# Attention's last steps in the middle of layer 1's slots, masks in three pieces, 25 products of zeros in place of 55

## The chip, the cores and the metric

The kernel runs on one core of a Trainium2 chip. The metric is device time in microseconds (us). The engines named here are PE (TensorE, matrix products; PEld is its weight load), DVE (VectorE), ACT (ScalarE), POOL (GpSimd) and SP (SyncE, which issues most of the DMAs). A line such as L615 is a line of the kernel before.

## The reference

Attention with sink keys and a sliding window, then two dense layers, all in float32 (B=2, H=8, S=768, D=64; window 128, 4 sink keys; d_model 512, d_ff 2048):

```python
scores = q @ k.T / sqrt(D)
keep   = (pos_k < n_sink) | ((rel >= 0) & (rel < window))
a      = softmax(where(keep, scores, -1e9))        # sum + 1e-9
x      = (a @ v).transpose(0, 2, 1, 3).reshape(1536, 512)
h = x @ w_in                                       # layer 1: 512 -> 2048 -> 512
P = a0 + a1*h + a2*h**2 + a3*h**3
Q = 1 + abs(b0)*abs(h) + abs(b1)*h**2
x = (P / (Q + 1e-6)) @ w_out
h = maximum(x @ w_in2, 0)                          # layer 2
out = (h * h) @ w_out2
```

n_sink and window are read at run time, so the masks are built on the chip.

## The kernel before, in words

**Arithmetic.** Every float32 operand of a large product is split into a rounded high half and a low half (names ending in h and l), and a product is three products of halves: high by high, high by low, low by high. The high half is made by ACT, the low half is the difference, made by DVE or POOL. The weights come as 64-bit numbers, packed; DVE turns a tile of them into float32 in three integer steps (L234, L240, L246: the weight conversion), and `w_fin` splits it (L267 on ACT, L268 on POOL).

**Attention.** 12 units of 128 tokens (6 for each batch entry) by 4 pairs of heads make 48 steps, n = 0 to 47, in a software pipeline. Step n issues: the exponentials of step n-1 (`expo`, ACT L434); the scores of step n (L404), ahead of which come some products of zeros (`fill`, L532) into the same PSUM tile; the masked maximum of those scores (DVE: from unit 1 on a predicated copy L410, then L417, which adds a mask m_0, m_1 or m_2); the transposes of step n-2's exponentials (`trans`, L454) and their copies with the window's triangles (POOL L463, L467); the product with v of step n-4 (`pv`, L494), and, every fourth step, the sink keys' share (L501, L503), the division (L506), the sink columns' transpose (`sinks_t`, L477) and, some steps later, the transposes of the finished unit (`xt`, L358) with its split into xh and xl (ACT L276, DVE L277). The scores lie in a PSUM tag S of two buffers, so the first product of step n+2, a zero where there is one, can start only when L417 of step n has read its tile. The table DENSE holds the number of zeros ahead of the scores of steps 0 to 11, DENSE_B that of steps 24 to 27, where the second batch entry begins. Another 14 stand ahead of everything (NW0).

**Masks.** `setup_first` makes m_0 (for unit 0), `setup_rest` the other masks: tri for L410, m_1 for unit 1 on and m_2. Its operations stand on DVE in step 0, behind the scores of that step. The helper `addm` is line 100. The split of q and k (`split`, L364 and L365) leaves the low half of unit 1 to DVE, that of later units to POOL. In step 1 POOL builds the block-diagonal mask bd of the sink values (`diagonal`, L329 and L333).

**Layers.** Layer 1 is computed in slots, one for each step k over tiles of d_ff and chunks of 512 tokens. Slot k issues in this order: the split of the function's value of k-2 (`act_c`: gh on ACT L672, gl on POOL L673), up to two `w_fin`, the rational function of k-1 (`act_b`), the first product of k+1 (`g1`, L615: 12 products of 512 columns into a PSUM tile T), ACT's and POOL's share of the function of k (`act_a`), the weight conversion until a due count (`w_until(due(k))`), and the second product of k-2 (`g2`, L690, 12 products into the S tiles). T has two buffers: g1(k+1) can start only when L653, the first DVE operation of `act_b` of k-1, has read g1(k-1)'s tile. `act_b` also has gaps in which up to one conversion step each is put on DVE. The list of what each engine executes is the order in which these functions issue.

**The seam.** The first chunks of x are finished before the last unit is. So g1(0) is issued in step 46, and in the steps NP+k (NP = 48) for k = 0 to 5 the whole slot k follows the product with v (`ahead`, L583). Steps 48 to 53 hold no scores of their own; they hold the last exponentials, transposes, products with v and `xt`: unit 10's in step 49, unit 11's in step 53, behind slot 5. Those `xt` and the sink transposes take the PSUM tag U, which the function's quotient (L657, L658) uses too. Weight conversion goes on in U until step 51's end, then in tag O. From slot 6 on, slots follow one another.

Of the kernel before, what the change touches and what calls it, by code (L numbers as in the profile page):

```python
# [15 lines left out]
P = 128  # L16
SK = 8
# [1 line left out]
TWO32 = 4294967296.0  # L19
WS = 3  # L20
NW0 = 14
DENSE = (4, 5, 6, 6, 4, 4, 3, 3, 2, 2, 2, 2)
DENSE_B = 3
QP = 1.0 + 1e-6

LEAST = 2.0 ** -15 * 1.125
# [12 lines left out]
def kernel(  # L39
# [59 lines left out]
    def addm(dst, src):  # L99
        nc.vector.tensor_scalar(out=dst, in0=src, scalar1=-1.0, scalar2=BIG, op0=ALU.add, op1=ALU.mult)  # L100
# [35 lines left out]
    def setup_rest(rel, win, snk, tmp, m_1, m_2, tri):  # L136
        nc.vector.tensor_scalar(out=tri, in0=rel[:, P:], scalar1=0.0, scalar2=None, op0=ALU.is_lt)
        nc.vector.tensor_tensor(out=tmp, in0=win[:, 0:P], in1=win[:, P:], op=ALU.max)
        for m in (m_1, m_2):
            addm(m[:, 0:P], tmp)  # L140
        addm(m_2[:, P:], snk[:, 0:SK])
        nc.vector.tensor_tensor(out=tmp[:, 0:SK], in0=snk[:, 0:SK], in1=win[:, 0:SK], op=ALU.is_gt)
        addm(m_1[:, P:], tmp[:, 0:SK])

    def setup_moe():
        nc.scalar.mul(out=na, in_=ab[:, 0:4], mul=-1.0)
# [21 lines left out]

    wst = {"load": 0, "int": 0, "fin": 0}
    wraw, wx, wt = {}, {}, {}  # L170
    conv = {"tag": "U"}
    NW = 2 * NF
    spare = [f"b{j}" for j in range(NW - 2 * NCH)]
    parts = {}
# [75 lines left out]
            w_load()  # L250

    def w_until(steps):
        while wst["int"] < min(steps, len(todo)):
            j, i = todo[wst["int"]]
            if jobs[j][0] == "c" and i == WS - 1 and len(wx) == 2:
                return
            w_step()
# [31 lines left out]
    def ps_t(tag=None, tail=False):  # L289
        if tail:  # L290
            return ps_s()[:, 0]
        if tag is None:
            tag = "U" if hq else "T"
        return ps.tile([P, 512], F32, tag=tag, name=tag, bufs=2 if tag == "T" else 1)


    def attention(ap, extra, ahead):
        kh = ap.tile([P, NPR, NS, BS], F32R, name="kh")
        kl = ap.tile([P, NPR, NS, BS], F32R, name="kl")
        m_0 = ap.tile([P, P], F32, name="m_0")  # L300
# [51 lines left out]
            nc.gpsimd.tensor_tensor(out=l, in0=m, in1=h.bitcast(F32), op=ALU.subtract)  # L352
            vs[b] = (h, l)

        def transposed(t):
            d = ps_t()
            for pr in range(NPR):
                nc.tensor.transpose(  # L358
                    d[:, pr * P:(pr + 1) * P], t[:, 2 * pr:2 * pr + 2, :].rearrange("p h d -> p (h d)"), ident
                )  # L360
            return d.rearrange("p (r t) -> p r t", r=NPR)

        def split(u, h, l, d, r=slice(0, NPR)):
            nc.scalar.copy(out=h[:, r], in_=d[:, r])  # L364
            (nc.vector if u == 1 or r.stop <= 2 else nc.gpsimd).tensor_tensor(  # L365
                out=l[:, r], in0=d[:, r], in1=h[:, r].bitcast(F32), op=ALU.subtract
            )

# [104 lines left out]
        def sinks_t(u):  # L473
            if u not in sk:
                return
            sd = ps_t()
            nc.tensor.transpose(sd[:, 0:P], sk.pop(u).rearrange("p j h s -> p (j h s)"), ident)  # L477
            st = ap.tile([P, P], F32R, name="st", bufs=2)
            hf = H * SK
            nc.scalar.copy(out=st, in_=sd[:, 0:P])  # L480
            nc.vector.tensor_tensor(out=st[hf:], in0=sd[hf:, 0:P], in1=st[hf:].bitcast(F32), op=ALU.subtract)
            sT[u] = st
# [33 lines left out]

        def xt(u):
            c, t0 = u // UPC, (u % UPC) * P
            d = transposed(ops.pop(("x", u)))
            split_ps(xh[c][:, :, t0:t0 + P], xl[c][:, :, t0:t0 + P], d)  # L520

        NP = NU * NPR
# [22 lines left out]
        prep_q(0, first)  # L545
        next(masks)
        prep_k(0, first)
        for n in range(NP + 6):
            u, pr = divmod(n, NPR)
            if 0 <= n - 1 < NP:  # L550
                expo(n - 1)
            if n < NP:
                scores(n)
            if n == 0:
                prep_q(0, second)
                prep_k(0, second)
                prep_q(0, others)
                prep_k(0, others)
                setup_rest(*next(masks), m_1, m_2, tri)
                sink_keys(0)  # L560
            if n == 1:
                bd = diagonal()
                moe = setup_moe()
            if pr == 0 and u + 2 < NU:
                load(u + 2)
            if pr == 1 and n < NP and u % NB == 0:
                load_sinks(u // NB)
            if 9 <= n < 20:
                next(moe, None)
            if 0 <= n - 2 < NP:  # L570
                trans(n - 2)
            if 0 <= n - 1 < NP and pr == 0:
                sinks(n - 1)
            if n >= 6 and pr == 2 and n // 4 - 1 < NU:
                sinks_t(n // 4 - 1)
                sums(n // 4 - 1)
            if 12 <= n <= NP and pr == 0:
                xt(n // 4 - 3)
            if n == NP + 1:
                xt(NU - 2)  # L580
            if 0 <= n - 4 < NP:
                pv(n - 4)
            if n in ahead:  # L583
                ahead[n]()
            if pr == 0 and u + 1 < NU:
                prep_q(u + 1)
            if pr == 1 and u + 1 < NU:
                prep_k(u + 1)
            if pr == 2 and u % NB == 0 and 0 < u < NU:
                sink_keys(u)  # L590
            if n in (5, NB * NPR + 3):
                sink_values(u // NB, bd)
            if n in (7, NB * NPR + 4):
                sink_split(u // NB)
            if n == NP + 5:
                xt(NU - 1)
            extra(n)

    def half(L, g):
# [21 lines left out]
    def layers(mp, due):  # L623
# [118 lines left out]

        K = len(steps)

        def slot(k):
            if 0 <= k - 2:
                act_c(k - 2)
            w_fin()
            w_fin()
            if 0 <= k - 1 < K:  # L750
                act_b(k - 1, lambda: w_until(min(due(k), wst["int"] + 1)))
            if k + 1 < K:
                g1(k + 1)
            if k < K:
                act_a(k)
            split_late()
            w_until(due(k))
            if 0 <= k - 2:
                g2(k - 2)
            if k == K + 1:  # L760
                finish(0)
                finish(1)
# [272 lines left out]
    with tc.tile_pool(name="ap", bufs=1) as ap:  # L1035
        def extra(n):
            if n == 3:
                for _ in range(NWR):
                    w_load()
            w_fin()  # L1040
            if n % 4 != 2:
                w_until(min(WS * NA, (WS * NA * (n - 4)) // (NU * NPR - 9)))
            if n == NU * NPR + EARLY - 1:
                conv["tag"] = "O"

        attention(
            ap, extra, {NU * NPR - 2: lambda: g1(0)} | {NU * NPR + k: lambda k=k: slot(k) for k in range(EARLY + 2)}
        )
    wp2 = main.enter_context(tc.tile_pool(name="wp2", bufs=1))
    wpool += [wp2] * (NW - NA)  # L1050
    for n in range(EARLY + 2, slots):
        slot(n)
        if n == KL + 3 * NF - 3:
            fl = verdict(mp)
# [43 lines left out]
```

## Time and profile before

| | |
|---|---|
| median of 3 runs | 664.74 us (663.9 to 664.88) |
| profiled execution, its own time | 662.6 us |
| span of that execution, first to last instruction | 660.9 us |
| mean granted TensorE clock | 0.996 of full speed |
| PE busy | 643.5 us, 97% of the span |
| DVE, ACT, POOL busy | 435.8, 365.5, 351.4 us |
| idle time of L615 behind L653 (whole span) | 6.4 us |

The time of the profiled execution is 1.7 us above its span, and 2.1 us below the median of the runs. Busy times are of instructions; PE's ends are modelled, and neighbouring matrix products overlap in the records, so that starts are to be compared rather than ends.

### The profile page before, as it was taken

Reading aid. Unit: us, or ns where it says so; the run is one execution under the profiler, and the core shown is the slowest. Engines: PE = TensorE matmul, PEld = TensorE weight load, DVE = VectorE, ACT = ScalarE, POOL = GpSimd, SP = SyncE. Lnnn points to the kernel's source line nnn. Section 1 sums busy time; section 2 is a strip of 40 time slices with the busy share of each in tenths; the row PEclk is TensorE's granted clock in tenths of the full one; section 3 lists DMA queues with packets and bytes.
Section 4 is the critical chain, followed back from the end, with each engine's and each line's share of the span. In section 5 each row is a group of like instructions: output and inputs, shape, how many; then the busy total and the mean of one; then the engine's idle time right before and its main releaser. Section 6 shows DMA issues by size and latency. Waiting matters only on the chain.

```text
span 660.9 us, 9330 instructions
## 1 busy us (share of the span) xinstructions
PE 643.5 (97%) x3189; PEld 525.5 (80%) x3189; DVE 435.8 (66%) x885; ACT 365.5 (55%) x783; POOL 351.4 (53%) x353
## 2 busy tenths in 40 slices
PE   8999999898999999999999999999999999999995
PEld 6788788776888888888888888888888888888884
DVE  5687786485989798867667679959766242441231
ACT  4788886755888778868759744333332132222220
POOL 4777785345776757667649547444443222222221
PEclk9999999999999999999999999999999999999998
DMA  7846642022322233212111135737637354430101
GB/s 196 228 117 174 168 114 65 0 64 64 97 94 66 96 96 96 64 33 64 32 33 32 64 127 171 247 110 248 222 122 250 97 190 128 144 111 1 63 1 69
DMA packets 64375, 72.06 MB, mean 109 GB/s; under 512 B 15424, under 2 KB 55360, under 8 KB 64320
## 3 DMA queue, kind: packets, MB, share of 16 engines
q1 hardware_dynamic: 64176, 71.38, 35.2%
q8 instruction: 27, 0.44, 0.3%
q14 instruction: 28, 0.23, 0.1%
q10 hardware_dynamic: 144, 0.00, 0.0%
HBM read 68.23 MB, written 3.15 MB: 108 GB/s over the span
## 4 chain that ended last, share of the span: by engine, by line
PE 92%; DVE 3%; issue 1%; POOL 1%; ACT 1%; DMA 1%; DVEq 0%; POOLq 0%; ACTq 0%
PE s L690 40%; PE T L615 33%; PE U L615 7%; PE O L494 5%; PE s L404 3%; PE T L454 2%; PE s L532 2%; DMA raw<-in_spans_dram 1%; PE O L503 1%; PE T L358 0%; DVE t L653 0%; PE O L501 0%; POOL w L268 0%; DVE ql L365 0%; ACT pe L434 0%
## 5 line engine op out<-in xcount | busy, mean ns | idle before, releaser
L615 PE MATMUL T<-xh,w 128*128 128x512 f32 x640 | 211.7, 392 | 6.4 <-DVE t L653 6.4
L673 POOL TENSOR_TENSOR gl<-g,gh 128x512 fp32r<-128x512 f32 x48 | 62.2, 1297 | 161.4 <-ACT gh L672 161.4
L615 PEld LDWEIGHTS T<-xh,w 128*128 128x128 f32 x640 | 120.2, 188 | 34.2 <-DVE t L653 7.6
L690 PE MATMUL s<-gh,w 128*128 128x512 f32 x384 | 126.2, 390 | 0.0
L615 PE MATMUL T<-xl,w 128*128 128x512 f32 x320 | 125.5, 392 | 0.0
L690 PE MATMUL s<-w,gh 128*128 128x512 f32 x384 | 119.6, 392 | 0.0
L673 POOL TENSOR_TENSOR gl<-t,gh 128x512 fp32r<-128x512 f32 x48 | 62.3, 1299 | 48.3 <-ACT gh L672 42.2
L636 POOL TENSOR_TENSOR t<-t,ah 128x512 f32<-128x512 f32 x48 | 62.3, 1297 | 48.2 <-ACT t L633 45.7
L690 PEld LDWEIGHTS s<-w,gh 128*128 128x128 f32 x384 | 72.0, 188 | 16.4
L268 POOL TENSOR_TENSOR w<-wx,w 128x512 fp32r<-128x512 f32 x64 | 83.1, 1300 | 2.9 <-ACT w L267 2.9
L690 PEld LDWEIGHTS s<-gh,w 128*128 128x128 f32 x384 | 72.1, 188 | 15.7
L672 ACT CAST gh<-g 128x512 fp32r<-128x512 f32 x48 | 29.9, 622 | 84.2 <-PE s L690 78.7
L690 PE MATMUL s<-w,gl 128*128 128x512 f32 x192 | 75.3, 392 | 0.0
L690 PE MATMUL s<-gl,w 128*128 128x512 f32 x192 | 75.2, 392 | 0.0
L615 PEld LDWEIGHTS T<-xl,w 128*128 128x128 f32 x320 | 60.1, 188 | 12.4
L661 DVE SCALAR_TENSOR_TENSOR t<-t,U 128x512 f32<-128x512 f32 x48 | 33.0, 687 | 30.1 <-ACT U L658 30.0
L672 ACT CAST gh<-t 128x512 fp32r<-128x512 f32 x48 | 29.8, 622 | 40.4 <-DVE t L665 32.4
L647 DVE TENSOR_TENSOR g<-r,T 128x512 f32<-128x512 f32 x32 | 21.8, 684 | 45.1 <-ACT r L640 45.1
L640 ACT ACTIVATE r<-T 128x512 f32<-128x512 f32 x32 | 19.2, 599 | 54.3 <-PE T L615 54.3
L494 PE MATMUL O<-vr,ph 128*128 128x64 f32 x352 | 44.7, 268 | 0.1
L494 PEld LDWEIGHTS O<-vr,ph 128*128 128x128 f32 x352 | 43.2, 192 | 0.4 <-issue 0.3
L434 ACT ACTIVATE pe<-ns,nmax 128x136 f32<-128x136 f32 (+1 forms) x96 | 38.3, 401 | 9.1 <-DVE nmax L417 8.6
(151 smaller groups left out, 1152.3 us busy)
## 6 DMA issues: line engine op xcount, KB each, us to landing
wr<-in_w_in_dram SPq DMA_DIRECT2D x54, 512.0 KB, 3.8
wr<-in_w_out_dram SPq DMA_DIRECT2D x52, 512.0 KB, 3.8
qr<-in_q_dram SPq DMA_DIRECT2D x12, 256.0 KB, 4.1
kr<-in_k_dram SPq DMA_DIRECT2D x12, 256.0 KB, 4.5
vr<-in_v_dram SPq DMA_DIRECT2D x12, 256.0 KB, 4.9
wr<-in_v_dram SPq DMA_DIRECT2D x6, 512.0 KB, 4.8
out_dram<-part SPq DMA_DIRECT2D x12, 256.0 KB, 2.1
vsc<-in_v_dram SPq DMA_DIRECT2D x4, 16.0 KB
```

The source lines that it names most:

```text
L268: nc.gpsimd.tensor_tensor(out=t[:, 1], in0=xf, in1=t[:, 0].bitcast(F32), op=ALU.subtract)
L404: nc.tensor.matmul(d[e][:, 0:w].rearrange("p (j n) -> p j n", n=bw), lhsT=ql[a][s, pr, :], rhs=kk[b][s, pr, slots, 0:bw], start=(a + b == ...
L434: nc.scalar.activation(out=t[:, e, 0:w], in_=ns[e][:, 0:w], func=ACTF.Exp, scale=-1.0, bias=nmax[:, ix:ix + 1], accum_out=rs[:, 2 * pr + e ...
L494: nc.tensor.matmul(o[:, h * D:(h + 1) * D], lhsT=pt[:, j, e], rhs=ld[u - 1 + j, "v"][:, h, :], start=(h == 0 and j == (i == 0)), stop=Fals ...
L615: nc.tensor.matmul(h, lhsT=wi[a][:, kk * P:(kk + 1) * P], rhs=(xh, xl)[b][c][:, kk, :], start=(kk == 0 and a + b == 0), stop=(kk == KD - 1 ...
L636: nc.gpsimd.tensor_tensor(out=t, in0=t, in1=ah, op=ALU.mult)
L640: nc.scalar.activation(out=r, in_=h, func=ACTF.Relu)
L647: nc.vector.tensor_tensor(out=g, in0=st.pop(k), in1=h, op=ALU.mult)
L661: nc.vector.scalar_tensor_tensor(out=t, in0=t, scalar=QP, in1=r0, op0=ALU.add, op1=ALU.mult)
L672: nc.scalar.copy(out=gh, in_=g)
L673: nc.gpsimd.tensor_tensor(out=gl, in0=g, in1=gh.bitcast(F32), op=ALU.subtract)
L690: nc.tensor.matmul(acc[L, g, c][m], lhsT=lh, rhs=rh, start=(f == f0 and a + b == 0), stop=(f == f1 and a == 1),)
```

## The change

**Slots and steps.** The loop over steps ends at 47. Slots 0 to 4 then each get a function `mid` that issues step NP+j after g1(j+1) and `act_a(j)`, and before the conversion and g2(j-2). g1(0) stays in step 46. xt of unit 11 is issued in step 52 in place of 53, into tag O; xt of unit 10 stays in step 49, and unit 11's sink transpose moves from step 50 to 49, and both go into tag S. Weight conversion is switched off from the end of step 48 to the end of step 52. The plain slots begin with 5.

**Masks.** `setup_rest` is a generator of three pieces, one each in steps 0, 1 and 2; m_2's first part is copied from m_1. `diagonal` and `setup_moe` move from step 1 to 2, the sink values from step 5 to 6 and their split from 7 to 8. The low halves of unit 1's q and k go to POOL.

**Zeros.** DENSE and DENSE_B are smaller: 2, 3, 3, 2 fewer in steps 1 to 4; 2, 1, 1, 2, 2, 2, 2 fewer in steps 5 to 11; 2 fewer in each of steps 24 to 27.

```diff
 NW0 = 14
-DENSE = (4, 5, 6, 6, 4, 4, 3, 3, 2, 2, 2, 2)
-DENSE_B = 3
+DENSE = (4, 3, 3, 3, 2, 2, 2, 2)
+DENSE_B = 1
 QP = 1.0 + 1e-6
...
         nc.vector.tensor_tensor(out=tmp, in0=win[:, 0:P], in1=win[:, P:], op=ALU.max)
-        for m in (m_1, m_2):
-            addm(m[:, 0:P], tmp)
-        addm(m_2[:, P:], snk[:, 0:SK])
+        yield
+        addm(m_1[:, 0:P], tmp)
         nc.vector.tensor_tensor(out=tmp[:, 0:SK], in0=snk[:, 0:SK], in1=win[:, 0:SK], op=ALU.is_gt)
         addm(m_1[:, P:], tmp[:, 0:SK])
+        yield
+        nc.vector.tensor_copy(m_2[:, 0:P], m_1[:, 0:P])
+        addm(m_2[:, P:], snk[:, 0:SK])
 
     def setup_moe():
...
-        while wst["int"] < min(steps, len(todo)):
+        while conv["on"] and wst["int"] < min(steps, len(todo)):
             j, i = todo[wst["int"]]
...
             nc.scalar.copy(out=h[:, r], in_=d[:, r])
-            (nc.vector if u == 1 or r.stop <= 2 else nc.gpsimd).tensor_tensor(
+            (nc.vector if r.stop <= 2 else nc.gpsimd).tensor_tensor(
                 out=l[:, r], in0=d[:, r], in1=h[:, r].bitcast(F32), op=ALU.subtract
...
                 return
-            sd = ps_t()
+            sd = ps_t(tail=u == NU - 1)
             nc.tensor.transpose(sd[:, 0:P], sk.pop(u).rearrange("p j h s -> p (j h s)"), ident)
...
             c, t0 = u // UPC, (u % UPC) * P
-            d = transposed(ops.pop(("x", u)))
+            d = transposed(ops.pop(("x", u)), ps_t("O") if u == NU - 1 else ps_t(tail=u == NU - 2))
             split_ps(xh[c][:, :, t0:t0 + P], xl[c][:, :, t0:t0 + P], d)
...
         prep_k(0, first)
-        for n in range(NP + 6):
+        bd, moe, rest = None, None, None
+
+        def step(n):
+            nonlocal bd, moe, rest
             u, pr = divmod(n, NPR)
             if 0 <= n - 1 < NP:
                 expo(n - 1)
@@ -556,9 +560,11 @@
                 prep_k(0, second)
                 prep_q(0, others)
                 prep_k(0, others)
-                setup_rest(*next(masks), m_1, m_2, tri)
                 sink_keys(0)
-            if n == 1:
+                rest = setup_rest(*next(masks), m_1, m_2, tri)
+            if n < 4:
+                next(rest, None)
+            if n == 2:
                 bd = diagonal()
                 moe = setup_moe()
             if pr == 0 and u + 2 < NU:
@@ -571,7 +577,7 @@
                 trans(n - 2)
             if 0 <= n - 1 < NP and pr == 0:
                 sinks(n - 1)
-            if n >= 6 and pr == 2 and n // 4 - 1 < NU:
+            if (n >= 6 and pr == 2 and n < NP) or n == NP + 1:
                 sinks_t(n // 4 - 1)
                 sums(n // 4 - 1)
             if 12 <= n <= NP and pr == 0:
@@ -580,22 +586,26 @@
                 xt(NU - 2)
             if 0 <= n - 4 < NP:
                 pv(n - 4)
-            if n in ahead:
-                ahead[n]()
+            if n == NP - 2:
+                g1(0)
             if pr == 0 and u + 1 < NU:
                 prep_q(u + 1)
             if pr == 1 and u + 1 < NU:
                 prep_k(u + 1)
             if pr == 2 and u % NB == 0 and 0 < u < NU:
                 sink_keys(u)
-            if n in (5, NB * NPR + 3):
+            if n in (6, NB * NPR + 3):
                 sink_values(u // NB, bd)
-            if n in (7, NB * NPR + 4):
-                sink_split(u // NB)
-            if n == NP + 5:
+            if n in (8, NB * NPR + 4):
+                sink_split(u // NB if n > 8 else 0)
+            if n == NP + 4:
                 xt(NU - 1)
             extra(n)
 
+        for n in range(NP):
+            step(n)
+        for j in range(5):
+            slot(j, lambda: step(NP + j))
 
 
     def half(L, g):
@@ -742,7 +752,7 @@
 
         K = len(steps)
 
...
                 act_a(k)
+            mid()
             split_late()
...
                 w_until(min(WS * NA, (WS * NA * (n - 4)) // (NU * NPR - 9)))
-            if n == NU * NPR + EARLY - 1:
-                conv["tag"] = "O"
-
-        attention(
-            ap, extra, {NU * NPR - 2: lambda: g1(0)} | {NU * NPR + k: lambda k=k: slot(k) for k in range(EARLY + 2)}
-        )
+            if n == NU * NPR:
+                conv["on"] = False
+            if n == NU * NPR + EARLY:
+                conv["tag"], conv["on"] = "O", True
+
+        attention(ap, extra)
     wp2 = main.enter_context(tc.tile_pool(name="wp2", bufs=1))
     wpool += [wp2] * (NW - NA)
-    for n in range(EARLY + 2, slots):
+    for n in range(EARLY + 1, slots):
         slot(n)
         if n == KL + 3 * NF - 3:
             fl = verdict(mp)
```

DVE near the start, from the making of tri to the maxima of step 1 (before) or step 2 (now). su holds the pieces from which masks are made (win, snk, tmp), m_105 is m_1, m_106 is m_2. Before:

```order
L137 TENSOR_SCALAR tri<-su 128x128
L138 TENSOR_TENSOR su<-su 128x128
L100 TENSOR_SCALAR m_105<-su 128x128
L100 TENSOR_SCALAR m_106<-su 128x128
L100 TENSOR_SCALAR m_106<-su 128x8
L142 TENSOR_TENSOR su<-su 128x8
L100 TENSOR_SCALAR m_105<-su 128x8
L365 TENSOR_TENSOR ql<-qr,qh 128x512
L417 ISA ns,nmax<-s,m_104 128x128
L417 ISA nmax 128x1
L417 ISA ns,nmax<-s,m_104 128x128
L417 ISA nmax 128x1
```

And now (L418 is the maximum, L144 the copy):

```order
L137 TENSOR_SCALAR tri<-su 128x128
L138 TENSOR_TENSOR su<-su 128x128
L418 ISA ns,nmax<-s,m_104 128x128
L418 ISA nmax 128x1
L418 ISA ns,nmax<-s,m_104 128x128
L418 ISA nmax 128x1
L100 TENSOR_SCALAR m_105<-su 128x128
L141 TENSOR_TENSOR su<-su 128x8
L100 TENSOR_SCALAR m_105<-su 128x8
L418 ISA ns,nmax<-s,m_104 128x128
L418 ISA nmax 128x1
```

The maxima of step 1 stood behind all masks and unit 1's ql; they now stand behind tri and tmp alone, and those of step 2 behind m_1.

POOL at the same place, from the low halves of unit 0's other pairs to the next unit. Before:

```order
L365 TENSOR_TENSOR kl<-kr,kh 128x2x128
L379 CAST kh<-kh 128x16x8
L379 CAST kl<-kl 128x16x8
L329 MEMSET bd 128x512
L333 AFFINE_SELECT bd<-bd 64x512 x4
L365 TENSOR_TENSOR ql<-qr,qh 128x512
L365 TENSOR_TENSOR kl<-kr,kh 128x4x128
```

And now:

```order
L366 TENSOR_TENSOR kl<-kr,kh 128x2x128
L380 CAST kh<-kh 128x16x8
L380 CAST kl<-kl 128x16x8
L366 TENSOR_TENSOR ql<-qr,qh 128x512
L366 TENSOR_TENSOR kl<-kr,kh 128x4x128
L331 MEMSET bd 128x512
L335 AFFINE_SELECT bd<-bd 64x512 x4
L366 TENSOR_TENSOR ql<-qr,qh 128x512
```

ql and kl of unit 1, 128x512 each, now stand on POOL ahead of the memory set and the four selections of bd.

DVE at the seam. L653 (now L663) with t frees a T tile; L661 to L665 (now L671 to L675) are the rest of the function; L234, L240, L246 (now L236, L242, L248) are conversion steps; L277 (now L279) makes xl of unit 11. Before, from the middle of the function of step 2 of layer 1 to the beginning of that of step 4:

```order
L663 SCALAR_TENSOR_TENSOR U<-t,U 128x512
L665 SCALAR_TENSOR_TENSOR t_2043<-t_2043,fa,U 128x512
L653 SCALAR_TENSOR_TENSOR t_2096<-t_2096,fa,T 128x512
L234 TENSOR_SCALAR O<-wr 128x512
L240 SCALAR_TENSOR_TENSOR O<-wr,O 128x512
L661 SCALAR_TENSOR_TENSOR t<-t,U 128x512
L246 SCALAR_TENSOR_TENSOR wx<-wr,O 128x512
L663 SCALAR_TENSOR_TENSOR U<-t,U 128x512
L234 TENSOR_SCALAR O<-wr 128x512
L665 SCALAR_TENSOR_TENSOR t_2096<-t_2096,fa,U 128x512
L240 SCALAR_TENSOR_TENSOR O<-wr,O 128x512
L653 SCALAR_TENSOR_TENSOR t_2148<-t_2148,fa,T 128x512
```

And now, from x of unit 11 to the function of step 4:

```order
L507 TENSOR_TENSOR x<-O,rs 128x512
L663 SCALAR_TENSOR_TENSOR t_2058<-t_2058,fa,T 128x512
L671 SCALAR_TENSOR_TENSOR t<-t,U 128x512
L673 SCALAR_TENSOR_TENSOR U<-t,U 128x512
L675 SCALAR_TENSOR_TENSOR t_2058<-t_2058,fa,U 128x512
L279 TENSOR_TENSOR xl_84<-O,xh_81 128x4x128
L236 TENSOR_SCALAR O<-wr 128x512
L242 SCALAR_TENSOR_TENSOR O<-wr,O 128x512
L248 SCALAR_TENSOR_TENSOR wx<-wr,O 128x512
L236 TENSOR_SCALAR O<-wr 128x512
L242 SCALAR_TENSOR_TENSOR O<-wr,O 128x512
L663 SCALAR_TENSOR_TENSOR t_2109<-t_2109,fa,T 128x512
```

Before, five conversion steps stood between the L653 of step 3 and that of step 4, among the rest of step 3's function, and unit 11's xl came later. Now the same five stand in a row behind xl of unit 11, and ahead of the L663 of step 4, which frees the tile that g1(6) takes.

## Rows read from the trace of the kernel before

**Rows 1.** The page, the span in 40 slices: granted TensorE clock in tenths
```profile
PEclk9999999999999999999999999999999999999998
```

**Rows 2.** Windows: busy us by engine, with instructions, granted clock, DMA share, GB/s
```profile
12.00:14.00 2.00, 0.70 (x4) 0.46 (x3) 2.00 (x8) 0.80 (x5) 1.41 (x2) 1.00 0.93 200
20.00:30.00 10.00, 10.00 (x76) 7.47 (x76) 7.57 (x33) 7.92 (x29) 8.46 (x15) 1.00 0.68 158
58.00:68.00 10.00, 10.00 (x74) 7.78 (x73) 6.09 (x24) 7.22 (x27) 7.52 (x15) 1.00 0.54 143
110.00:170.00 60.00, 53.45 (x259) 42.80 (x258) 36.82 (x61) 37.44 (x67) 26.82 (x26) 1.00 0.13 37
170.00:640.00 470.00, 470.00 (x2055) 385.06 (x2054) 310.20 (x489) 241.84 (x403) 240.26 (x187) 1.00 0.34 109
```

**Rows 3.** Timeline, PE at the start: start, us, what, [idle before <-releaser]
```profile
13.53 1.63 PE L532 MATMUL s<-wz 128*128 128x512 f32 x6 [1.30 <-DVE nmax L417]
15.09 0.33 PE L404 MATMUL s<-kh,qh 64*128 64x128 f32 x2
...
16.86 0.39 PE L404 MATMUL s<-kh,qh 64*128 64x272 f32 x2
```

**Rows 4.** Timeline, DVE at the start
```profile
6.78 0.23 DVE L100 TENSOR_SCALAR m<-su 128x128 f32<-128x128 f32 x1
...
9.65 0.62 DVE L137 TENSOR_SCALAR tri<-su 128x128 int32<-128x128 f32 x1
...
10.44 1.23 DVE L100 TENSOR_SCALAR m<-su 128x128 f32<-128x128 f32 x3
...
11.76 0.61 DVE L100 TENSOR_SCALAR m<-su 128x8 f32<-128x8 f32 x1
...
12.88 0.28 DVE L417 CUSTOM_DVE_ANT_0 ns<-s,m 128x128 f32<-128x128 f32 x1
```

**Rows 5.** Timeline, POOL at the start
```profile
7.42 0.73 POOL L365 TENSOR_TENSOR ql<-qr,qh 128x256 fp32r<-128x256 f32 x1 [5.57 <-ACT qh L364]
...
9.66 0.53 POOL L329 MEMSET bd<- 128x512 f32 x1
10.26 3.22 POOL L333 TENSOR_SCALAR_AFFINE_SELECT bd<-bd 64x512 f32<-64x512 f32 x4
18.93 1.28 POOL L365 TENSOR_TENSOR ql<-qr,qh 128x512 fp32r<-128x512 f32 x1 [5.46 <-ACT qh L364]
```

**Rows 6.** Timeline, PE in step 8 (with two zeros) and step 12 (with none)
```profile
26.07 1.00 PE L494 MATMUL O<-vr,ph 128*128 128x64 f32 x8
26.88 0.72 PE L532 MATMUL s<-wz 128*128 128x512 f32 x2
27.52 0.40 PE L404 MATMUL s<-kh,qh 64*128 64x272 f32 x2
...
37.62 1.00 PE L494 MATMUL O<-vr,ph 128*128 128x64 f32 x8
38.55 0.40 PE L404 MATMUL s<-kh,qh 64*128 64x272 f32 x2
```

**Rows 7.** Waits, 110 to 170 us: us in total, times, longest
```profile
PE T L615 <- DVE t L653: 6.4, 5, 2.1
```

**Rows 8.** Timeline, PE at unit 11's transposes
```profile
152.18 0.60 PE L358 MATMUL U<-ident,x 128*128 128x128 f32 x4
154.83 0.50 PE L615 MATMUL T<-xh,w 128*128 128x512 f32 x1 [2.06 <-DVE t L653]
```

**Rows 9.** Timeline, ACT at the same place
```profile
152.81 0.59 ACT L276 CAST xh<-U 128x512 fp32r<-128x512 f32 x1 [6.07 <-PE U L358]
```

**Rows 10.** Timeline, DVE at the same place, and a conversion step earlier
```profile
139.04 0.70 DVE L240 SCALAR_TENSOR_TENSOR O<-wr,O 128x512 int32<-128x512 int32 x1
...
153.43 0.69 DVE L277 TENSOR_TENSOR xl<-U,xh 128x512 fp32r<-128x512 f32 x1 [5.37 <-ACT xh L276]
154.04 0.74 DVE L653 SCALAR_TENSOR_TENSOR t<-t,fa,T 128x512 f32<-128x512 f32 x1
```

More of the change, by code (lines that the diff above doesn't have):

```diff
@@ L170 @@
     wraw, wx, wt = {}, {}, {}
-    conv = {"tag": "U"}
+    conv = {"tag": "U", "on": True}
     NW = 2 * NF
@@ L294, in ps_t, with attention @@
         return ps.tile([P, 512], F32, tag=tag, name=tag, bufs=2 if tag == "T" else 1)
-    def attention(ap, extra, ahead):
+    def attention(ap, extra):
         kh = ap.tile([P, NPR, NS, BS], F32R, name="kh")
@@ L353, in sink_split, with transposed @@
             vs[b] = (h, l)
-        def transposed(t):
-            d = ps_t()
+        def transposed(t, d):
             for pr in range(NPR):
@@ L743, in layers, with slot @@
         K = len(steps)
-        def slot(k):
+        def slot(k, mid=lambda: None):
             if 0 <= k - 2:
```

## The prediction, made before the changed kernel ran

> **What bounds the kernel now.** I read the page's clock line and busy shares first, then windows by stretch, then the timelines of PE, DVE and POOL where PE is not full, and the waits of the stretch where attention hands over to layer 1.
>
> From 170 to 640 us PE is busy for 470.00 of 470 us at granted clock 1.00 [rows 2]. The change touches no instruction there except through its starting time, so whatever it wins or loses ahead of 170 us is carried to the end unchanged. Three stretches are left. At the start, from 12 to 14 us, PE works for 0.70 of 2.00 us while DVE is full [rows 2]: the zeros ahead of step 3's scores wait 1.30 us for the maxima of step 1 [rows 3]. From 20 to 30 us, and around the second batch entry from 58 to 68 us, PE is the full engine with 10.00 of 10, though part of its work is products of zeros; POOL, next to it, has 8.46 and 7.52 [rows 2]. At the seam, 110 to 170 us, PE is busy for 53.45 of 60 [rows 2]: of the missing 6.55 us, 6.4 are five waits of layer 1's first product for the DVE operation that frees its T tile, the longest 2.1 us [rows 7].
>
> **The price of a zero.** Six zeros ahead of step 3 put the scores 1.56 us behind the first of them (13.53 to 15.09) [rows 3], two zeros in step 8 put them 0.64 behind (26.88 to 27.52) [rows 6]: (1.56 - 0.64) / 4 = 0.23, or 0.26 by the six alone (1.56 / 6); I take 0.235 where some zeros remain. Taking a step's last two is worth less than its 0.64, since the first score then pays the change of tile itself: from the product with v to the scores it is 26.07 to 27.52, 1.45 us, with two and 37.62 to 38.55, 0.93, with none [rows 6], so 0.52.
>
> **Term 1, the start (steps 1 to 4: 10 zeros, the masks, unit 1's low halves).** Before, step 1's maxima begin at 12.88 and let PE go on at 13.53, step 3's scores come at 15.09 and step 4's at 16.86 [rows 3, 4]. The maxima waited for nothing but DVE's own queue: tri, three mask operations (1.23 us), two small ones and unit 1's ql. In the new order they stand behind tri and tmp only. If these ran undisturbed, at about 0.25 each from 9.65 on [rows 4], they would be done by 10.2 to 10.4 and the maxima would follow. The path from the maxima's start X to step 3's scores is 0.65 (12.88 to 13.53) plus 1.56 less three zeros, 0.85, so X + 1.5; and from there to step 4's scores 1.77 (15.09 to 16.86) less two zeros, 1.3. With X = 10.4 PE's own queue is nearly as late (it has to end steps 1 and 2), I get scores at 12.2 and 13.6, a gain of 3.3 us: the upper end.
>
> Against it stands what POOL now does at that moment. A mask operation of 128x128 takes 0.23 us at 6.78, where POOL is idle (it had been for 5.57 us at 7.42), but three take 1.23, 0.41 each, at 10.44, and one of 128 by 8 takes 0.61 at 11.76, while POOL runs the selections (3.22 us from 10.26); tri took 0.62 while POOL ran its memory set of 0.53 from 9.66 [rows 4, 5]. That is, DVE's small operations on SBUF ended about when the POOL operation beside them did. In the new order unit 1's ql and kl, at 1.28 us each [rows 5], stand on POOL from about 9.66 to 12.2, exactly beside tri and tmp. If those end with them, X is 12.25 and step 3's scores come at 13.75. Step 2's maxima then stand behind step 1's (0.5) and three mask operations, two of them beside selections at 0.6 (1.4 together), so they start at about 14.15 and end by 14.65; PE goes on at 14.8 and step 4's scores come at 14.8 + 0.6 = 15.4. Gain 16.86 - 15.4 = 1.4 us, the value I take, since the rows beside a running POOL are nearer to the new case than the one beside an idle one. If each mask operation waits for a whole 1.28 us operation of POOL, nearly all of it goes: the lower end is 0.
>
> [...]
>
> The bd mask and the sink values only come a step later; POOL idles for 5.46 us ahead of 18.93 [rows 5], and that covers them, at no cost. If they were late, the first sink product, in step 10, would wait, which the lower end of term 2 covers.
>
> **Term 2, steps 5 to 11 (12 zeros).** Steps 5, 6 and 7 lose two, one and one: 4 x 0.235 = 0.94. Steps 8 to 11 lose their last two: 4 x 0.52 = 2.08. Together 3.0 us, if PE stays the limit. With 10 us of PE shrunk to about 8, POOL's 8.46, ACT's 7.92 and DVE's 7.57 would be beyond or near it [rows 2], though a part of POOL's and DVE's load there is weight work that can drift later. I keep 3.0 with a lower end of 1.5.
>
> **Term 3, steps 24 to 27 (8 zeros).** One of three stays in each: 8 x 0.235 = 1.9 us. PE is full there and the next engine has 7.52 of 10 [rows 2], which covers a tenth or two less. Lower end 1.
>
> **Term 4, the seam.** The same steps are issued, PE's work is the same, and only the five waits can change. By following the new orders by hand: g1(2) is as before, its L663 still behind xl of unit 9, which I put at the mean of the five, 6.4 / 5 = 1.28 [rows 7]. g1(3) now stands behind unit 10's transposes and xl: also 1.28, and the transposes themselves wait some 0.5, an estimate, for an S tile that a copy of ACT's must free (one of twice the columns takes 0.59 [rows 9]). g1(4) has g2(0) ahead of it now, 12 products more, and DVE no longer has x of unit 11 ahead of the freeing operation: 0. g1(6) is the bad one. Before, unit 11's chain ran transposes 152.18, ACT 152.81, DVE 153.43, L653 154.04, g1 154.83, with 0.63, 0.62, 0.61 and 0.79 from each to the next [rows 8 to 10]. Now five conversion steps of 0.70 [rows 10] stand between the last two, 3.5 us: 0.63 + 0.62 + 0.61 + 3.5 + 0.79 = 6.15 from the transposes to g1(6). PE has the transposes (0.60) and g2(2) meanwhile, 12 products at 470 / 2055 = 0.229 [rows 2], 2.74: it waits 2.8 us. g1(7), with 2.06 before [rows 8], no longer has transposes in front: 0. Sum 1.28 + 1.28 + 0.5 + 2.8 = 5.85 against 6.55, a gain of 0.7 us. Ends: +4, if the pile is covered or the steps before it leave DVE early; -1.5, if g1(4) or g1(7) keeps a wait of its own.
>
> **Sum.** 1.4 + 3.0 + 1.9 + 0.7 = 7.0 us. The profiled execution would go from 662.6 to 655.6 and its span from 660.9 to 653.9. The median of the runs lies 2.1 above that execution, so the forecast is 664.74 - 7.0 = 657.7 us; the likeliest case by itself spans 656.5 to 659.5.
>
> **Rivals.** (a) POOL does not hold DVE up: term 1 is 3.3, and the time 655.8. For it: the rows show ends that coincide, not the cause. Against it: tri and four mask operations all did so [rows 4, 5]. (b) The seam gives nothing or loses, because the pile of conversion steps costs more than the waits that go: 7.0 - 0.7 - 1.5 = 4.8 won, 659.9. For it: 3.5 us of DVE work on the path, none of which was there before. Against it: three of five waits lose their reason. (c) The zeros of steps 5 to 11 were no limit: other engines set the pace, term 2 is 1.5 or less and the time 659.2 or more. For it: POOL's 8.46. Against it: PE had no idle time at all there. (d) The seam is better than by hand, g1(6) hardly waits: the wait of 2.8 goes too, 654.9. [...]
>
> [...]
>
> **Chances.** Main case 0.42, (a) 0.20, (b) 0.16, (c) 0.08, (d) 0.06, (e) short 0.04 and long 0.04. The range has to hold 8 in 10: from 654.6, near (d), to 661.2, beyond (b) and (c). A measurement of this kernel tells 0.2%, 1.3 us, from no change, so faster means below 663.4: all of the main case and (a) to (d) but a few parts, 0.91. Between 663.4 and 666.1 lies a mixture of (b) with (c), 0.04; slower is (e) long and whatever I overlooked at the start, 0.05.
>
> **What would show it.** In the changed profile: step 4's scores near 15.4 us and tri's end beside POOL's ql or kl (13.6 and a short tri would show (a)); step 12's scores 4.4 us earlier than 38.55, near 34.1; no zeros' wait for maxima longer than 0.3 us in steps 5 to 11, else (c); g1(6) waiting about 3 us for DVE behind five conversion steps, and no wait for g1(4) and g1(7); the waits of the first product near 5.5 us in all; the clock line still all nines. Wrong would be a start that gains more than 3 us, a seam with waits of over 8 or under 3 us, or any stretch at clock 0.5.

## The result, and the profile after

The changed kernel takes 658.02 us (median of 4 runs, three of them from 656.07 to 658.09) against 664.81: a ratio of 0.989, interval 0.9866 to 0.9914. Run again beside the experiments on another chip it gave 656.52 and 0.9881 (0.9857 to 0.9906). It is faster, and the predicted 657.7 lies 0.3 us from the first median. Some executions of most kernels here, the one before too, have a mean granted TensorE clock of 0.884 to 0.982, where the others have 0.988 to 0.998 (by the windows of the four of them that were profiled it was 0.50 for some 17 to 58 us); the ratios leave out runs over 1.5% above their kernel's fastest, and a median is given only for kernels with one such run at most.

The two profiled executions differ less than the medians: the span went from 660.9 to 656.2 us, 4.7 in place of 6.8. Windows of the changed kernel first, as in [rows 2] (busy us of PE, PEld, DVE, ACT, POOL, then the granted clock):

```profile
12.00:14.00 2.00, 1.51 (x11) 0.80 (x9) 1.93 (x6) 0.54 (x4) 1.86 (x4) 1.00 0.91 203
20.00:30.00 10.00, 9.57 (x81) 7.78 (x80) 8.50 (x36) 8.88 (x37) 9.43 (x15) 1.00 0.94 236
110.00:170.00 60.00, 54.30 (x247) 44.20 (x246) 40.71 (x63) 39.44 (x67) 29.47 (x27) 0.94 0.16 47
170.00:640.00 470.00, 470.00 (x2054) 385.02 (x2054) 307.39 (x485) 238.03 (x396) 237.37 (x185) 1.00 0.33 108
```

From 170 us on nothing changed. PE at the start is twice as busy. From 20 to 30 us PE now has small gaps, with POOL at 9.43. At the seam the granted clock, 1.00 before, is 0.94.

PE's timeline shows where the time went (start, us, what, [idle before <-releaser]); the row at 34.34 answers to the 38.55 of [rows 6]:

```profile
11.73 0.94 PE L533 MATMUL s<-wz 128*128 128x512 f32 x3 [0.20 <-DVE nmax L418]
14.31 0.70 PE L533 MATMUL s<-wz 128*128 128x512 f32 x2 [0.80 <-DVE nmax L418]
14.95 0.39 PE L405 MATMUL s<-kh,qh 64*128 64x272 f32 x2
...
28.62 0.44 PE L455 MATMUL T<-ident,pe 128*128 128x128 f32 x2 [0.36 <-ACT pc L463]
...
34.34 0.39 PE L405 MATMUL s<-kh,qh 64*128 64x272 f32 x2
...
113.67 0.50 PE L625 MATMUL T<-xh,w 128*128 128x512 f32 x1 [1.22 <-DVE t L663]
...
117.36 0.66 PE L359 MATMUL s<-ident,x 128*128 128x128 f32 x4 [0.35 <-ACT pc L463]
...
120.07 0.50 PE L625 MATMUL T<-xh,w 128*128 128x512 f32 x1 [1.22 <-DVE t L663]
...
142.81 0.79 PE L625 MATMUL T<-xh,w 128*128 128x512 f32 x1 [2.92 <-DVE t L663]
...
151.20 0.39 PE L625 MATMUL T<-xh,w 128*128 128x512 f32 x1
...
162.13 0.39 PE L625 MATMUL T<-xh,w 128*128 128x512 f32 x1
```

Step 4's scores moved from 16.86 [rows 3] to 14.95: 1.91 us. The row at 38.55 moved to 34.34, 4.21 us, so 2.30 more. (The prediction calls that row step 12; counted from step 4 it is step 14's, and the one called step 8 is step 9's. The same rows were compared, so no number changes.) The score rows of step 30, behind the second batch's zeros, stand at 73.69 before and 67.63 after: 6.06, so 1.85 more. Scores of step 47 stand at 111.66 and 105.42: 6.24. But the first product of slot 9, at 166.94 before, stands at 162.13: 4.81. The seam lost 1.43 us of what had been won.

The reason stands at 142.81. g1(6) waits 2.92 us, and behind the wait one product takes 0.79 and the next 0.63 where 0.50 and 0.39 are usual: from g1(6) to g1(7) it is 151.20 - 142.81 = 8.39 us, while from g1(8) at 156.66 to g1(9) it is 5.47. That costs 2.9 us. The window around it, and the seam's wait in all, as in [rows 7]:

```profile
140.00:150.00 10.00, 7.18 (x19) 5.72 (x20) 9.26 (x15) 6.88 (x12) 5.06 (x4) 0.66 0.47 122
```

```profile
PE T L625 <- DVE t L663: 5.3, 3, 2.9
```

The granted clock is 0.66 over these 10 us, and 0.50 from 142 to 148: PE ran that part at half the clock of the 10 us on either side (1.00), behind the longest idle time of the seam.

### The profile page after: what moved, and what is told of

Same layout as the page of the kernel before. It is cut to its first block, busy times and chain, and to the rows that moved or that the text cites. A ratio compares the mean times of both kernels' runs of the same rounds, so it can differ in the third digit from the quotient of the medians.

```text
span 656.2 us, 9270 instructions
## 1 busy us (share of the span) xinstructions
PE 639.5 (97%) x3159; PEld 523.3 (80%) x3159; DVE 435.7 (66%) x883; ACT 365.4 (56%) x783; POOL 354.2 (54%) x355
## 4 chain that ended last, share of the span: by engine, by line
PE 93%; DVE 3%; POOL 1%; ACT 1%; DMA 1%; issue 1%; SPq 0%; DVEq 0%; POOLq 0%; ACTq 0%
PE s L700 40%; PE T L625 34%; PE U L625 7%; PE O L495 4%; PE s L405 3%; PE T L455 2%; PE T L533 1%; DMA vsc<-in_v_dram 1%; PE s L533 1%; PE T L359 1%; PE O L504 0%; PE O L502 0%; DVE xl L279 0%; DVE ns L418 0%; DVE t L663 0%
## 5 line engine op out<-in xcount | busy, mean ns | idle before, releaser
L671 DVE SCALAR_TENSOR_TENSOR t<-t,U 128x512 f32<-128x512 f32 x48 | 32.9, 686 | 32.4 <-ACT U L668 32.1
L269 ACT CAST w<-wx 128x512 fp32r<-128x512 f32 x64 | 39.5, 617 | 8.8 <-DVE wx L248 8.8
```

Of the source, the lines that this page charges most:

```text
L269: nc.scalar.copy(out=t[:, 0], in_=xf)
L671: nc.vector.scalar_tensor_tensor(out=t, in0=t, scalar=QP, in1=r0, op0=ALU.add, op1=ALU.mult)
```

## The experiments

Theory: zeros on PE's path cost their own time; the masks' early pieces let PE reach it; the seam's new order saves waits but piles five conversion steps ahead of g1(6), and that wait brings a fall of the clock which gives the saving back. The rivals are named run by run, and whether such a wait always brings a fall is taken up in the last section.

### The parts alone

**The zeros alone**, on the kernel before:

```diff
-DENSE = (4, 5, 6, 6, 4, 4, 3, 3, 2, 2, 2, 2)
-DENSE_B = 3
+DENSE = (4, 3, 3, 3, 2, 2, 2, 2)
+DENSE_B = 1
```

> The kernel before with the new tables of zeros alone (25 in place of 55). My theory: zeros on PE's path cost their own time. Steps 5 to 11 gain the 2.3 us that the changed kernel's trace shows between step 4's and step 12's scores, steps 24 to 27 the 1.85 seen there; at the start step 1's maxima stay at 12.88, PE goes on at 13.53, and with three and two zeros step 4's scores come at about 15.7 in place of 16.86, 1.2. Sum 5.3 us, so about 659.5, with scores of step 12 near 35.0. Rival: the zeros of steps 1 to 11 only fill time in which PE would wait for the others, so the time falls by the 1.85 of steps 24 to 27 or little more, 662 to 663. Other rival: fewer zeros let TensorE's clock fall in the first 30 us; then a stretch at 0.5 shows there and the time is not lower.

Ratio 0.9926 (0.9894 to 0.9959): 4.9 us, near the 5.3 expected and over the rival's 2 to 3. At the start the maxima stand where they did, but PE with fewer zeros comes to them sooner:

```profile
13.66 1.62 PE L532 MATMUL s<-wz 128*128 128x512 f32 x3 [2.01 <-DVE nmax L417]
```

The wait grew from 1.30 [rows 3] to 2.01: without the masks' early pieces part of what the zeros give up is spent waiting.

The other rival does not fall with the ratio. In this profiled execution, which took 678.12 us, the granted clock goes down within that wait (1.00 to 13.0 us, 0.50 from 13.5 us on) and stays down until 61 us; the zeros' 1.62 us above and the rows behind them run at that 0.50 and price nothing.

```profile
20.00:30.00 10.00, 10.00 (x44) 7.18 (x45) 3.28 (x17) 4.81 (x20) 4.99 (x7) 0.50 0.68 168
```

The runs behind the ratio, too, lie at mean clocks of 0.988 to 0.992 (before: 0.989 to 0.996 but for two). So 4.9 us is what fewer zeros win where the clock does not fall like this at the start; whether it falls there more often with fewer zeros is neither shown nor excluded.

**The masks alone**, on the kernel before, with the three pieces as in the change:

```diff
-                setup_rest(*next(masks), m_1, m_2, tri)
                 sink_keys(0)
-            if n == 1:
+                rest = setup_rest(*next(masks), m_1, m_2, tri)
+            if n < 4:
+                next(rest, None)
+            if n == 2:
...
-            (nc.vector if u == 1 or r.stop <= 2 else nc.gpsimd).tensor_tensor(
+            (nc.vector if r.stop <= 2 else nc.gpsimd).tensor_tensor(
...
```

> The kernel before with the masks in three pieces, unit 1's low halves on POOL and bd a step later; zeros and seam as before. My theory: step 1's maxima go at about 11.1 in place of 12.88, then PE's own queue with its six zeros is the limit; step 4's scores come near 15.4 in place of 16.86, and the time falls by 1.4 us, to 663.4. Rival: with all zeros on PE's path the masks were hidden but for the wait of 1.30, and POOL's 2.7 us of ql and kl push DVE as far back as before: under 0.5 us, 664.4 or more.

PE's timeline has step 4's scores at

```profile
15.42 0.40 PE L406 MATMUL s<-kh,qh 64*128 64x272 f32 x2
```

as expected (15.4; 16.86 before), 1.44 us. The ratio, 0.9988 (0.994 to 1.0036), can't tell so little; at equal mean clock, 0.996, three runs gave 661.48 to 661.51 and one run of the kernel before 662.75, 1.25 us. The rival's 0.5 falls by the row; the times alone would not decide it.

This kernel keeps the old seam, and its trace shows a fall of the clock there as well, behind g1(4)'s wait of 1.51 us at 141.72. The kernel before has the same wait, 1.51 at 135.68, and no fall.

```profile
140.00:150.00 10.00, 8.49 (x31) 6.75 (x31) 9.54 (x15) 5.38 (x9) 3.92 (x4) 0.83 0.18 49
```

**The seam alone**, written as an edit of the changed kernel, whose masks and zeros go back to those of before:

```diff
-DENSE = (4, 3, 3, 3, 2, 2, 2, 2)
-DENSE_B = 1
+DENSE = (4, 5, 6, 6, 4, 4, 3, 3, 2, 2, 2, 2)
+DENSE_B = 3
...
+                setup_rest(*next(masks), m_1, m_2, tri)
                 sink_keys(0)
-                rest = setup_rest(*next(masks), m_1, m_2, tri)
-            if n < 4:
-                next(rest, None)
-            if n == 2:
+            if n == 1:
...
```

> The kernel before with the seam's new order alone; masks and zeros as before. My theory: waits of 5.3 us of layer 1's first product for DVE (2.9 of them at g1(6), behind five conversion steps) in place of 6.4, which wins 1.5 us with all that moves; but where the wait at g1(6) is followed by products at half the clock, as in the changed kernel's trace (granted 0.66 from 140 to 150 us), it loses 2.9. So the span is 659.4 without the fall and 662.3 with it, and the time is between -1.5 and +1.4 us of the kernel before: no clear gain. Rival: the seam is where the gain of the median (6.8 us) that the two traces do not show (4.7) comes from, and this kernel is 2 us faster or more.

Ratio 0.9967 (0.9933 to 1.0002): no clear gain, as expected; the rival's 2 us lie inside the interval and are not excluded by the time alone. The next run bears on the same question.

Its trace speaks against a part of the theory. The waits are the same, 2.92 for g1(6) at 174.55, but here no fall of the clock follows, and from g1(6) to g1(7) it is 5.62 us:

```profile
PE T L621 <- DVE t L659: 5.3, 3, 2.9
170.00:180.00 10.00, 7.08 (x32) 5.48 (x31) 9.72 (x16) 5.21 (x10) 4.64 (x4) 1.00 0.36 106
```

So the pile makes the wait, but the wait does not bring the fall each time. (In this execution the granted clock had been 0.50 from 80 to 130 us, and 0.89 and 0.71 in the 10 us ahead of and behind that, before the 2.92.)

**Masks and zeros without the seam**: the kernel before with both edits above.

> The kernel before with the new masks and the new zeros; the seam as before. My theory: the seam's new order by itself wins 1.5 us in waits and gives 2.9 back to the clock, so all of the change's gain is zeros and masks: 1.9 + 2.3 + 1.85 = 6.05 us off the kernel before, a span of 654.9 and a time of 656.6 where the clock falls no more than there, that is the changed kernel's time within 1.3 us. Rival: the new order is worth its own time and this kernel is 1.5 us or more slower than the changed one, 658.5 to 660.

657.99 us (656.85 to 658.34), ratio 0.9893 (0.9848 to 0.9938): the same as the changed kernel's 0.989 and 0.9881. The seam's new order as made is worth nothing that can be measured. Its span was 655.1 (expected 654.9), with a small fall of the clock behind the wait of unit 11's transposes, which is the 2.06 of [rows 8]:

```profile
148.49 0.72 PE L620 MATMUL T<-xh,w 128*128 128x512 f32 x1 [2.06 <-DVE t L658]
```

```profile
140.00:150.00 10.00, 7.95 (x35) 6.35 (x34) 3.06 (x5) 3.94 (x8) 3.53 (x3) 0.93 0.14 46
150.00:160.00 10.00, 10.00 (x41) 8.10 (x40) 9.05 (x14) 6.89 (x12) 6.81 (x7) 0.90 0.33 105
```

The same wait had no fall behind it in the profiled execution of the kernel before. So the old seam has falls of its own; how often the clock falls in either seam, one trace of each kernel does not tell.

**The changed kernel with the 55 zeros** (the two tables as before, nothing else):

> The changed kernel with the 55 zeros of before. My theory: all of the zeros' time comes back where masks and seam are as changed: step 4's scores at 15.4 and step 12's at about 37.1 in place of 14.95 and 34.34, steps 24 to 27 another 1.85: 4.6 us, 661 to 662.5. Rival: the zeros hold the clock up and the runs with them show a higher mean clock, 0.996 or more, so that only 1 to 3 us are lost: 658 to 660.

Step 4's scores stand at 15.44 and step 14's at 37.13 (called step 12 there), as expected to 0.05 us. Ratio 0.9945 (0.9921 to 0.9969) against 0.9881 for the changed kernel beside it: the zeros cost 4.3 us. The rival that more zeros hold the clock up falls: its profiled execution has the clock down at 70 to 100 us,

```profile
70.00:100.00 30.00, 28.96 (x185) 25.03 (x183) 21.19 (x80) 21.37 (x76) 20.76 (x31) 0.72 0.55 149
```

and in two of nine runs the mean clock was over 0.995, in the changed kernel in two of six.

### The pile and the clock

**The changed kernel again:**

> The changed kernel once more, beside the others: 656 to 658.5 us. My theory: its runs differ by how far TensorE's granted clock falls behind g1(6)'s wait (657.94 at a mean clock of 0.993, 656.07 at 0.995), so its times and mean clocks lie on one line, about 0.7 us for 0.001. Rival: the times differ at the same clock, for a reason that the clock does not show.

From 658.09 at a mean clock of 0.992 to 654.89 at 0.998, some 0.5 us for 0.001 (0.7 was expected), and two runs at 0.995 are 0.77 apart: the clock tells much of the spread, not all. The wait at g1(6) was 2.94 and the granted clock from 140 to 150 us 0.83. From g1(6) to g1(7) it is 6.93 us, so this fall cost 1.5 where the first trace's cost 2.9.

**No conversion in slot 4** (spread):

```diff
+    wtiles[12], wtiles[13] = wtiles[13], wtiles[12]
...
             slot(j, lambda: step(NP + j))
+        conv["on"] = True
...
+        if k == EARLY:
+            return WS * NA
         if k < KB:
-            return WS * NA + (WS * (READY - NA) * (k + 2 - EARLY)) // (KB + 1 - EARLY)
+            return min(WS * READY, WS * (NA + k - EARLY))
...
-                conv["tag"], conv["on"] = "O", True
+                conv["tag"] = "O"
```

> The changed kernel with no conversion in slot 4: it resumes in slot 5, three steps a slot, each in a gap of the function there (two weight tiles change places so that each comes in time). My theory: the five steps in a row are the whole cause of g1(6)'s wait of 2.92 us; it goes to 0.2 or less, waits of the first product fall from 5.3 to about 2.5, and with the wait the fall of the granted clock from 142 to 149 us goes, which cost another 2.9 (8.39 us from g1(6) to g1(7) where 5.45 is usual). The run whose trace fell would be 652, the median 652 to 654. Rival: conversion three times a slot beside the function makes DVE late in slots 5 to 8, or the weight tiles late for g2, and the waits come back there: 656 to 658. Other rival: the fall has nothing to do with the wait: 654 to 655 with the fall still in the trace.

652.19 us (651.99 to 653.95), ratio 0.9823 (0.9801 to 0.9846), 4.3 us under the changed kernel on the same chip; span 650.3, expected 650.4. PE and clock over the stretch of the pile:

```profile
140.00:150.00 10.00, 10.00 (x46) 8.27 (x45) 9.31 (x15) 7.24 (x13) 6.02 (x6) 1.00 0.30 101
```

```profile
PE T L627 <- DVE t L665: 2.4, 2, 1.2
```

g1(6) waits no more, the two waits of 1.2 stay, PE is full and the clock up. Wait and fall went together, 5.9 us of span (656.2 to 650.3), as 2.92 + 2.9 says; against the second trace of the changed kernel, 654.6, it is 4.3, as 2.94 + 1.5 says. DVE's 9.31 shows the steps still done there, in gaps that PE does not feel. Both rivals fall, the second with a reserve: in the seam alone the fall stayed away though the wait was there. That spread's six runs lie at mean clocks of 0.996 to 0.998, where the changed kernel beside it has 0.992 to 0.998, speaks for the wait as the cause.

**Three steps in slot 4 in place of five** (conversion resumes in slot 4 as in the changed kernel; the tiles change places as in spread):

```diff
+        if k == EARLY:
+            return WS * NA + 3
         if k < KB:
-            return WS * NA + (WS * (READY - NA) * (k + 2 - EARLY)) // (KB + 1 - EARLY)
+            return min(WS * READY, WS * (NA + k - EARLY + 1))
```

> The changed kernel with three conversion steps in slot 4 in place of five, the rest three a slot. My theory: g1(6) waits 2.92 - 2 x 0.73 = 1.5 us, and the clock stays up behind it, as it did behind the 2.06 us at the same place in the kernel before: gain 1.4 + 2.9, 653.5 to 655.5. Rival: a wait of 1.5 leaves the fall as it is: gain 1.4 alone, 656 to 657.

```profile
141.55 0.50 PE L626 MATMUL T<-xh,w 128*128 128x512 f32 x1 [1.49 <-DVE t L664]
```

1.49 us, as expected (1.5), and the clock is 1.00 from 140 to 150. 654.58 us, ratio 0.9842 (0.9815 to 0.9869): between the two others, where the theory put it (653.5 to 655.5). Its last product starts 1.80 us later than spread's (644.51 and 642.71); the rest of the 3.2 us between their spans lies behind the last product.

### POOL's share at the start

**Unit 1's low halves back on DVE**, all else as changed:

```diff
-            (nc.vector if r.stop <= 2 else nc.gpsimd).tensor_tensor(
+            (nc.vector if u == 1 or r.stop <= 2 else nc.gpsimd).tensor_tensor(
```

> The changed kernel with unit 1's low halves of q and k back on DVE; all else as changed. My theory: in the changed kernel DVE's tmp (1.37 us at 9.79) and first mask operation (1.34 at 11.50) end when POOL's ql and kl beside them do; without these on POOL both take 0.6 or less, step 1's maxima come at about 10.7 in place of 11.08 although ql now stands ahead of them, and step 4's scores at about 14.3 in place of 14.95. Rival: DVE's operations are slow for a reason of their own and now carry 1.3 us more: tmp and the mask operation still take over 1 us and step 4's scores come at 15.5 or later.

DVE and POOL of the changed kernel, as [rows 4] and [rows 5]:

```profile
9.66 0.21 DVE L137 TENSOR_SCALAR tri<-su 128x128 int32<-128x128 f32 x1
9.79 1.37 DVE L138 TENSOR_TENSOR su<-su 128x128 f32<-128x128 f32 x1
11.08 0.28 DVE L418 CUSTOM_DVE_ANT_0 ns<-s,m 128x128 f32<-128x128 f32 x1
...
11.50 1.34 DVE L100 TENSOR_SCALAR m<-su 128x128 f32<-128x128 f32 x1
```

```profile
9.69 1.33 POOL L366 TENSOR_TENSOR ql<-qr,qh 128x512 fp32r<-128x512 f32 x1
10.97 1.33 POOL L366 TENSOR_TENSOR kl<-kr,kh 128x512 fp32r<-128x512 f32 x1
12.24 0.52 POOL L331 MEMSET bd<- 128x512 f32 x1
```

and DVE in the experiment, whose start lay 0.36 us later:

```profile
10.55 0.22 DVE L138 TENSOR_TENSOR su<-su 128x128 f32<-128x128 f32 x1
10.69 1.13 DVE L366 TENSOR_TENSOR ql<-qr,qh 128x512 fp32r<-128x512 f32 x1
...
12.16 0.25 DVE L100 TENSOR_SCALAR m<-su 128x128 f32<-128x128 f32 x1
...
13.16 1.15 DVE L366 TENSOR_TENSOR kl<-kr,kh 128x512 fp32r<-128x512 f32 x1
```

The same two operations, tmp and the first mask operation, take 1.37 and 1.34 us beside POOL's ql and kl (the second ends only with the memory set behind kl), and 0.22 and 0.25 without: the hold-up is shown, and the rival on it falls. But step 4's scores came at 15.50, 15.14 less the later start, and not at 14.3 (its one run took 658.24 us): on DVE ql and kl took 1.13 and 1.15, where the kernel before has 0.68 and 0.71. POOL's selections ran beside ql in both (10.62 to 13.78 here, 10.26 to 13.48 before), so what makes the two longer here is not shown. Time is lost on either side: the move to POOL won 0.2 us at most. The maxima, which read one input from PSUM, were not held up: they took 0.28 us at 11.08, while POOL's kl ran (10.97 to 12.30), and 0.29 at 15.79 in the kernel before, where POOL was idle.

### A version faster than both

Spread, and no zeros behind step 3:

```diff
-DENSE = (4, 3, 3, 3, 2, 2, 2, 2)
-DENSE_B = 1
+DENSE = (4, 3, 3, 3)
+DENSE_B = 0
```

> The kernel with conversion spread over the slots, and no zeros behind step 3: 8 fewer in steps 4 to 7, 4 fewer in steps 24 to 27. My theory: steps 4 to 7 lose their last two, 0.52 each, 2.1 us, and steps 24 to 27 their last, about 0.3 each, 1.2, less where DVE, ACT and POOL, at 8.5 to 9.4 of 10 us there, become the limit: 1.5 to 3 us off the 652.2 of the spread kernel, 649.2 to 650.7, with the clock up. Rival: the other engines have the pace there already and nothing is won, 652. Other rival: this is where the zeros held the clock up; it falls in the first 60 us, and the time is above 655.

650.12 us (648.64 to 650.62), ratio 0.9768 (0.9723 to 0.9813): 2.1 us under spread's median, taken on another chip, as expected (1.5 to 3). The clock was 1.00 in each 10 us of the first 60, so in this execution the last 12 zeros behind step 3 had no use left. The limit of it is seen at 20 to 30 us, where PE now waits for DVE and ACT, with POOL full:

```profile
21.40 1.08 PE L496 MATMUL O<-vr,ph 128*128 128x64 f32 x8 [0.61 <-DVE x L508]
...
27.34 0.44 PE L456 MATMUL T<-ident,pe 128*128 128x128 f32 x2 [0.48 <-ACT pc L464]
```

```profile
20.00:30.00 10.00, 8.91 (x76) 7.29 (x75) 8.45 (x36) 8.76 (x38) 9.94 (x16) 1.00 0.99 259
110.00:130.00 20.00, 17.49 (x82) 14.15 (x83) 9.79 (x17) 14.17 (x26) 7.83 (x8) 0.91 0.00 0
```

The second row shows a fall of the clock in this execution, behind g1(3)'s wait of 1.22 us at 117.36. From g1(3) to g1(4) it is 8.10 us where spread has 6.51, so this fall cost 1.6.

## Why the prediction was right, and where it was not

**Term 1, 1.4 predicted, 1.9 measured.** Step 4's scores came at 14.95 in place of 15.4. DVE's operations were held up beside POOL's, as the term took it (tmp 1.37 us beside POOL's ql, 0.22 without), and (a) was wrong, but the gain came out near by two errors that work against each other. The step that failed is X = 12.25: tri slipped in ahead of POOL's ql (0.21 us at 9.66, ql at 9.69), so only tmp was held, for one POOL operation and not two, and the maxima began at 11.08. The kernel before had shown such a case, which the prediction counted with the held ones: the three operations at 10.44 in [rows 4] are two of 128x128 and one of 128x8, and the second of them began at 10.92, as one of POOL's selections ended (10.93), and took 0.21. The second price was too low: the first mask operation took 1.34, not 0.6.

**Term 2, 3.0 and 2.3.** Its condition, that PE stays the limit, held but for small waits: ACT's copy cost 0.36 at 28.62, and from step 8's scores to step 9's it is 2.10 us (21.86 to 23.96) where 2.31 less 0.52, 1.79, was reckoned. That is a little of (c).

**Term 3, 1.9 and 1.85.** The price of a zero, 0.235, was right.

**Term 4, +0.7 and -1.4.** The waits came almost as worked out: g1(2) 1.22, g1(3) 1.22, the S tile 0.35, g1(4) none, g1(6) 2.92 for 2.8. What failed is the sentence that only the waits can change there: behind g1(6)'s wait the clock fell, 2.9 us. Without it the seam would have won 1.5: 0.85 is PE's idle time, 6.55 us before and 5.70 from step 47's scores to g1(9) now, and the rest no run explains. In the second trace, where the fall cost 1.5, the seam comes out even: from step 47's scores to g1(9) it is 55.25 us (105.38 to 160.63), and 55.28 before (111.66 to 166.94). The prediction's own sign of being wrong, a stretch at clock 0.5, is there from 142 to 148 us. The chances give a short and a long fall of the clock, (e), 0.04 each; no row of the kernel before shows one, with 1.00 in every window of [rows 2]. The runs showed falls that cost 2.9 and 1.5 us here, behind the pile of conversion steps that was reckoned as a wait alone, and one from 13.5 to 61 us in the zeros alone.

**The sum.** By the two traces the terms are 1.9 + 2.3 + 1.85 + 0.2 (steps 30 to 47) - 1.4 = 4.8, for a span that fell by 4.7; 7.0 was predicted. That the medians differ by 6.8 all the same comes from the other side: the profiled execution of the kernel before, 662.6 us at a mean clock of 0.996, was the fastest of its kind, and most of its runs are at 0.991 to 0.994 and 662.9 to 665.3. Falls of the clock were in the median of before as well; where each of them fell no trace of that kernel tells; three experiments with its seam show falls there, behind waits of 1.51 (masks alone) and 2.05 to 2.06 us (zeros alone; masks and zeros). So the hit of 0.3 us owes something to two errors that cancel: I left the clock out of the new seam, and out of the old kernel's runs.

## What to carry to other kernels

A wait ahead of a dense engine is to be priced with what follows it: here 2.9 us of waiting were followed, in four traces of five, by a fall of the clock that cost another 1.5 to 2.9, and spreading five steps of a third engine over the next slots won both back. When small work is moved to a second engine, look whether it holds up the first engine's operations at that moment: here two of them took 1.37 and 1.34 us in place of 0.22 and 0.25, and of the 2.3 us that ql and kl took on DVE the move won 0.2. Zeros put in to keep an engine busy should be tried away one group at a time once the waits that they bridged are gone.

## What the runs showed of the hardware

The clock fell more often behind longer waits of PE, 4 times of 5 behind 2.9 us and once of 20 behind 1.2, but the length alone does not decide it. These are the waits of 1.2 us and more of layer 1's first product for DVE at the seam, in the twelve profiled executions, and how often the granted clock fell behind them:

| wait, us | times | with a fall | where |
|---|---|---|---|
| 2.92 to 2.94 | 5 | 4 | not in the seam alone |
| 2.05 to 2.06 | 4 | 2 | zeros alone; masks and zeros |
| 1.49 to 1.51 | 5 | 1 | masks alone |
| 1.21 to 1.22 | 20 | 1 | the last kernel |

Behind the 2.9 us at g1(6), the clock over the 10 us around it was 0.66 in the first trace of the changed kernel and 0.83 in the three others. In three traces, all with the 55 zeros (masks alone, seam alone, the changed kernel with 55 zeros), the clock also fell near 77 us (0.83 to 0.89 from 70 to 80 us, 0.50 from 80 to 90), where no wait of PE since 58 us had been longer than 0.36, and stayed at 0.50 for 15 us or more; the kernel before has the same small waits there and no fall. What decides between these is open.
